# Writing out the order of the first batch's groups as a list in a fused attention and router kernel

## The chip, the cores and the metric

The kernel runs on one core of one Trainium2 chip. The metric is the device time of one execution in microseconds (us), as the median of several executions. Five engines work side by side, each through its own instructions in the order in which they were written out: TensorE (PE, matrix products and transposes, with its weight loads shown apart as PEld), VectorE (DVE), ScalarE (ACT), GpSimd (POOL) and SyncE (SP, which here only issues transfers). An engine that reaches an instruction whose inputs are not ready waits there, and everything behind it on that engine waits too.

## The reference, cut to what matters

```python
def phi(x):                       # S1, S2: 8 x 32 sketches
    a = einsum('rd,bhsd->bhsr', S1, x)
    b = einsum('rd,bhsd->bhsr', S2, x)
    return (a[..., :, None] * b[..., None, :]).reshape(..., 64)

q_p, k_p = phi(q), phi(k)         # batch 4, heads 4, sequence 1088, head size 32
kv = einsum('bhsf,bhsd->bhfd', k_p, v)
z = k_p.sum(axis=2)
attn = (q_p @ kv) / (q_p . z + 1e-6)

x = attn as 4352 rows of 128      # the heads of a token side by side
logits = normed(x) @ normed(expert_emb).T / tau       # 8 experts
e, gate = argmax and softmax's maximum of logits
out[row] = gate[row] * (relu(x[row] @ w1[e]) @ w2[e])  # w1: 128 x 1024, w2: 1024 x 128
```

Attention has no softmax: the keys and values of a head are first summed into one 64 x 32 matrix, so all keys have to be through before the first query is answered. Each row then goes through one of eight experts.

## The kernel before, in words

**Two halves.** The batch of four is taken in two halves of two (`m` = 0 and 1; the names of the steps of the first half end in 0, "ktr0"). A half has 17 tiles of 128 positions. They are taken in groups of four, called 0 to 3, and a last tile of one, called r. The changed lines are about the first half alone. What a group goes through, step by step:

- `ktr0 g`, `qtr0 g` (helper `turned`): PE transposes the group's keys or queries, four 128x128 transposes into one of two PSUM buffers of the name `ps_t`, and ACT copies the result to SBUF (kT, qT; rows of line 377).
- `kab0 g` (helper `sketch`, line 394): PE multiplies the turned keys by both sketches into the PSUM bank `ps_ab`. `kb0 g` (line 400): ACT copies the second factor out. `kp0 g` (helper `features`, line 410): DVE multiplies the two factors, 128x1024 numbers.
- `pairs g` (line 558): for the queries PE computes the two factors already repeated as the 64 products need them, into two PSUM buffers `ps_big`, of which there are exactly two. The 16 products of a group write both buffers in turn, the first buffer first. `sec g 0`, `sec g 1` (function `seconds`, line 567): ACT copies the second factors of each buffer to SBUF, 128x512 each. `prod g 0`, `prod g 1` (function `prods`, line 570): DVE multiplies the first factors, still in PSUM, by the copied second ones into `held`. The next group's `pairs` can write a buffer only when the `prod` on it is done.
- `kv0 g` (line 472): PE sums the products of keys and values in the PSUM bank `ps_acc`.
- The last tile r has short forms of these: `kab0 r`, `kb0 r`, `kp0 r` for the keys, `qab0 r`, `qb0 r`, `qp0 r` for the queries.

**Steps that belong to no group.** `constants` (DVE memsets), `sketches` (`turn_sketches`), `iotas` (POOL writes index tables, DVE converts them in eleven instructions, lines 282 to 302; they serve the router later), `norm emb` and `scale emb` (the norm of the expert embeddings: ACT squares, POOL takes the root by a power, DVE scales and lays them out, lines 318 to 334), `clear 0` and `clear 1` (POOL zeroes the two `kz` tiles, line 310), and `ktr 0`, the first turned keys of the second half.

**What sets the order.** Nothing is planned by a scheduler: within `emit` the functions are called in an order that is fixed by numbers. `put_at(tick)` returns `put(after, rank, f)`, which files the function f under the tick plus `after`, and `emit` calls all of a tick in order of rank. Group i of the first half is filed around tick i; from tick 4 on the list `ORDER` names the steps one by one, and the expert blocks follow from tick 10. The ranks of the first half's groups come out as this order before the change:

```
constants; ktr0 0; sketches; qtr0 0;
kab0 0; kb0 0; pairs 0; sec 0 0; ktr0 1; sec 0 1; kp0 0; qtr0 1; prod 0 0; prod 0 1;
kab0 1; kb0 1; pairs 1; sec 1 0; ktr0 2; sec 1 1; kp0 1; qtr0 2; prod 1 0; prod 1 1; iotas; clear 0;
kab0 2; kb0 2; pairs 2; sec 2 0; ktr0 3; sec 2 1; kv0 0; kp0 2; qtr0 3; prod 2 0; prod 2 1; kv0 1; ktr0 r; qtr0 r; norm emb; clear 1;
kab0 3; kab0 r; kb0 3; kb0 r; pairs 3; qab0 r; sec 3 0; qb0 r; sec 3 1; scale emb; ktr 0; kp0 3; kp0 r; prod 3 0; prod 3 1; qp0 r; kv0 2;
kv0 3; kv0 r;  then ORDER: tremb; total0; ktr 1; trkv0; ...
```

`tremb` turns the scaled embeddings (PE) and lays them out in `en_blk` (`place_emb`, DVE, line 344); `kve0` (line 496) is the first product that needs `en_blk`; from it come the columns of `kz` that give a query its logits (`nd 0 0` and on, line 610).

Of the kernel before, what the change touches and what calls it, by code (L numbers as in the profile page):

```python
# [27 lines left out]
NC = S // HALF  # L28
# [37 lines left out]
def kernel(  # L66
# [242 lines left out]
    def clear(m):  # L309
        nc.gpsimd.memset(kz[m], 0.0)  # L310
# [40 lines left out]
    TABLE1 = 12  # L351


    ORDER = """
tremb; total0; ktr 1; trkv0; kvT0; kab 0 ab; kb 0; trqp0r; kve0; kab 1 acc; kz0; ktr 2; nd 0 0; kb 1; ktr 3;
kp 0; nd 0 1; kab 3 ab; kb 3; x 0 0; nd 0 2; kab 2 t; x 0 1; kp 1; x 0 2; kb 2; kp 3; kv 0; nd 0 3; ktr r;
# [8 lines left out]
    steps = {}  # L365
# [19 lines left out]
    def sketch(ps, t, n):  # L385


        for h in range(H if n > 1 else 1):
            for u in range(2):
                r = slice(u * HALF, (u + 1) * HALF)  # L390
                if n == 1:
                    nc.tensor.matmul(ps[r, :H * 2 * R], t[:, r], Sblk.rearrange("p g r -> p (g r)"), start=True, stop=True)
                else:
                    nc.tensor.matmul(ps[r].rearrange("p (g h r) -> p g h r", h=H, r=2 * R)[:, :, h],  # L394
                                     t[:, h * P + u * HALF:h * P + (u + 1) * HALF], Sblk, start=True, stop=True)
        return ps[:, :n * H * 2 * R].rearrange("p (g t r) -> p g t r", t=2, r=R)
# [18 lines left out]
    def ab_bank(tick, n, u):  # L415


        if (tick, n) not in ab_ps:
            if n == 1:
                ps = ps_small()[:, :2 * n * HALF].rearrange("p (u n) -> p u n", u=2)  # L420
            else:
                ps = ps_one("ab").rearrange("p (u n) -> p u n", u=2)
            ab_ps[tick, n] = ps
        return ab_ps[tick, n][:, u, :n * HALF]

    def ab_next(kind, n, bank):

        if n == 1:
            return ab_ps[kind][:, 4 * HALF:5 * HALF]
        ab_ps[kind] = ps_small() if bank == "t" else ps_one(bank)  # L430
        return ab_ps[kind][:, :n * HALF]
# [2 lines left out]
        for bank in ("ab", "acc", "t"):  # L434
            steps[f"{name} {bank}"] = lambda bank=bank: f(bank)

    def keys(m, c0, c1, put=None):
        n = c1 - c0
        s = {}

# [1 line left out]
            s["kT"] = turned(None if n == 1 else k_sb[m][:, :, c0:c0 + 4], k_rest[m], n, "kT")  # L442

        def ab(bank=None):
            s["ab"] = sketch(ab_bank(put.tick, n, 1) if put else ab_next("k", n, bank), s["kT"], n)

        both = m == 1
        by_pool = m == 1 and c0 > 0
# [53 lines left out]
        if m == 1:  # L502
# [3 lines left out]
            if n == 1:  # L506
                steps.update({"total": total, "trkv": tr_kv, "kvT": kvT, "kve": lambda: kve(0), "kz": lambda: kve(1)})
            return
        put(-1, 50.6 if n > 1 else 55.5, tr)
        put(0, 49.8, ab)  # L510
        put(0, 49.85, b)
        put(0, 53, prod)
        first = c0 >= NC - 5
        put(*((2, 51) if c0 == 0 else (1, 47) if first else (1, 55)), kv)
        if c1 == NC:
            steps.update({"total0": total, "trkv0": tr_kv, "kvT0": kvT, "kve0": lambda: kve(0), "kz0": lambda: kve(1)})

    xg, lg, spare, turned_q = {}, {}, {}, {}

    def queries(m, c0, c1, put=None):  # L520
        n = c1 - c0
        w = n * P
        s = {}
# [9 lines left out]
            s["qT"] = turned(None if n == 1 else q_sb[m][:, :, c0:c0 + 4], q_rest[m], n, "qT")  # L533

        def ab(bank=None):
            s["ab"] = sketch(ab_bank(put.tick, n, 0) if put else ab_next("q", n, bank), s["qT"], n)

        both = m == 1

# [23 lines left out]
        def seconds(j):  # L563
            if j == 0:
                s["b"] = tile_of(n, [P, 2, w], "qpT")
                s["qpT"] = held[:, c0 // 4].rearrange("p (a n) -> p a n", a=2)
            nc.scalar.copy(s["b"][:, j], s["big"][j].rearrange("p j n -> p (j n)")[:, 2 * P:6 * P])

        def prods(j):
            nc.vector.tensor_mul(s["qpT"].rearrange("p a (j n) -> p j a n", j=4)[:, 2 * j:2 * j + 2],  # L570
                                 bview(s["big"][j], [[6 * P, 2], [P, 2], [1, P]]),
                                 s["b"][:, j].rearrange("p (j a n) -> p j a n", j=2, a=2))
# [60 lines left out]
        if n > 1:  # L633
            steps.update({f"nd {m} {step}": nd, f"x {m} {step}": x})
        if m == 0:
            put(-1, 53 if n > 1 else 55.6, tr)
            if n == 1:
                put(0, 50, ab)
                put(0, 50.5, b)
                put(0, 54, prod)  # L640
                steps.update({"trqp0r": tr_qp, "qpT0r": qpT})
            else:
                put(0, 50, pairs)
                for j in range(2):
                    put(0, 50.5 + 0.2 * j, lambda j=j: seconds(j))
                    put(0, 54, lambda j=j: prods(j))
        else:
            steps.update({f"qtr {step}": tr, f"qb {step}": b, f"qp {step}": prod,
                          f"trqp {step}": tr_qp, f"qpT {step}": qpT})
            by_bank(f"qab {step}", ab)  # L650
# [390 lines left out]
    def put_at(tick):  # L1041
        def put(after, rank, f):
            at.setdefault(tick + after, []).append((rank, len(at.get(tick + after, ())), f))
        put.tick = tick
        return put

    for i, group in enumerate(GROUPS):
        for tiles in group:
            for m in range(NM):
                keys(m, *tiles, put_at(i) if m == 0 else None)  # L1050
                queries(m, *tiles, put_at(i) if m == 0 else None)
    put_at(-1)(0, 40, more_constants)
    put_at(-1)(0, 52.9, turn_sketches)
    put_at(1)(0, 55, iotas)
    put_at(2)(0, 60, norm_emb)
    put_at(3)(0, 51, scale_emb)
    put_at(3)(0, 52, steps["ktr 0"])
    put_at(1)(0, 91, lambda: clear(0))
    put_at(2)(0, 91, lambda: clear(1))

    count, rest, others = plan_early()
    find, high, low, sums, tokens, *_ = table(0, 1, lambda: early["key"])
# [120 lines left out]
```

## Time and profile before

| what | us |
|---|---|
| median of 3 executions | 207.26 (206.97 to 208.28) |
| profiled execution, its own time | 206.99 |
| its span, first to last instruction | 205.2 |
| PE busy, share of the span | 194.0, 95% |
| ACT busy | 103.0, 50% |
| DVE busy | 87.8, 43% |
| POOL busy | 106.8, 52% |
| start of the first transposes (`ktr0 0`) | 4.34 |
| `tremb`, first step of ORDER | 24.71 |
| first gather of rows for the experts (POOL) | 50.13 |

The profile shows one execution. Each row of its timeline gives the start, the length, the engine, the line and the tiles of an instruction or of several alike, and in brackets how long its engine had sat idle before it and what ended that wait. Matrix products are pipelined, so rows of PE overlap by some tenths of a us; starts are the better guide. The chain of work that ended last is followed back from the last instruction; each piece of it is what the next one waited for. The core's granted TensorE clock has a mean of 0.998 of full speed, so a changed clock is no theme of the profile before.

The first 25 us hold the first half's groups. Loads of k, q and v fill the transfer engines from 4.5 us on (busy shares of 0.95 to 1.15 between 4.5 and 25 us), issued by SP without a wait on any computation.

### The profile page before, as it was taken

Reading aid. Unit: us, or ns where it says so; the run is one execution under the profiler, and the core shown is the slowest. Engines: PE = TensorE matmul, PEld = TensorE weight load, DVE = VectorE, ACT = ScalarE, POOL = GpSimd, SP = SyncE. Lnnn points to the kernel's source line nnn. Section 1 sums busy time; section 2 is a strip of 40 time slices with the busy share of each in tenths; the row PEclk is TensorE's granted clock in tenths of the full one; section 3 lists DMA queues with packets and bytes.
Section 4 is the critical chain, followed back from the end, with each engine's and each line's share of the span. In section 5 each row is a group of like instructions: output and inputs, shape, how many; then the busy total and the mean of one; then the engine's idle time right before and its main releaser. Section 6 shows DMA issues by size and latency. Waiting matters only on the chain.

```text
span 205.2 us, 6948 instructions
## 1 busy us (share of the span) xinstructions
PE 194.0 (95%) x2586; PEld 183.3 (89%) x2586; DVE 87.8 (43%) x378; ACT 103.0 (50%) x294; POOL 106.8 (52%) x137
## 2 busy tenths in 40 slices
PE   7989998999897999999999999999999999998991
PEld 7658788798787999999999999999999999997891
DVE  6577847788948368931221312212122122122100
ACT  2656461436373546534654555546555465776330
POOL 4010035302743567666777767677676776753033
PEclk9999999999999999999999999999999999999999
DMA  4999899568354996645465665665656794592000
GB/s 132 334 274 315 179 311 292 165 221 248 70 216 136 318 341 175 184 155 154 146 199 177 165 210 156 181 196 154 210 161 176 229 313 152 200 268 114 3 26 24
DMA packets 28162, 39.42 MB, mean 192 GB/s; under 512 B 5738, under 2 KB 21366, under 8 KB 28130
## 3 DMA queue, kind: packets, MB, share of 16 engines
q1 hardware_dynamic: 25776, 34.23, 56.7%
q0 software_dynamic: 2304, 4.74, 7.6%
q8 instruction: 22, 0.36, 0.7%
q14 instruction: 10, 0.08, 0.1%
q10 hardware_dynamic: 50, 0.01, 0.0%
HBM read 34.37 MB, written 4.73 MB: 191 GB/s over the span
## 4 chain that ended last, share of the span: by engine, by line
PE 88%; DVE 3%; ACT 2%; DMA 2%; issue 2%; POOL 0%; POOLq 0%; DVEq 0%
PE ps_big L983 27%; PE ps_acc L1019 14%; PE ps_ab L1019 14%; PE ps_acc L472 4%; PE ps_big L610 4%; PE ps_big L988 4%; PE ps_t L375 4%; DMA xs<-rows,dst_i 2%; PE ps_t L935 2%; PE ps_big L558 2%; PE ps_acc L1022 2%; PE ps_ab L1022 2%; PE ps_t L801 2%; PE ps_acc L105 1%; PE ps_ab L394 1%
## 5 line engine op out<-in xcount | busy, mean ns | idle before, releaser
L983 PE MATMUL ps_big<-xTb,wb 128*128 128x128 f32 x512 | 62.8, 276 | 0.0
L1031 POOL DMA_INDIRECT out_dram<-y,dst_i x36 | 37.5, 1043 | 44.4 <-ACT sq L996 20.1
L983 PEld LDWEIGHTS ps_big<-xTb,wb 128*128 128x128 f32 x512 | 59.7, 192 | 0.5 <-issue 0.2
L991 ACT ACTIVATE hT<-ps_big 128x1024 f32<-128x1024 f32 x36 | 36.8, 1024 | 37.2 <-PE ps_big L983 36.4
L929 POOL DMA_INDIRECT xs<-rows,dst_i x36 | 37.6, 1043 | 18.9 <-DVE dst_i L816 10.9
L937 DVE COPY xTb<-ps_t 128x128 f32<-128x128 f32 x29 | 8.4, 291 | 61.9 <-PE ps_t L935 61.9
L1019 PE MATMUL ps_acc<-w_sb,hT 128*128 x256 | 31.3, 275 | 0.1
L1019 PE MATMUL ps_ab<-w_sb,hT 128*128 x256 | 31.2, 275 | 0.0
L1019 PEld LDWEIGHTS ps_acc<-w_sb,hT 128*128 128x128 f32 x256 | 29.9, 192 | 0.1
L1019 PEld LDWEIGHTS ps_ab<-w_sb,hT 128*128 128x128 f32 x256 | 29.9, 192 | 0.0
L997 POOL TENSOR_TENSOR norm<-norm,half_c 128x1 f32<-128x1 f32 x36 | 21.3, 595 | 3.6 <-ACT sq L996 3.0
L1010 DVE TENSOR_SCALAR gate<-gate 128x1 f32<-128x1 f32 x36 | 5.5, 152 | 22.1 <-ACT probs L1007 22.0
L1028 ACT ACTIVATE y<-ps_acc,gate 128x128 f32<-128x128 f32 x18 | 6.6, 367 | 14.3 <-PE ps_acc L1019 10.9
L410 POOL TENSOR_TENSOR kp<-both 128x1024 f32<-128x1024 f32 (+1 forms) x4 | 6.5, 1619 | 11.8 <-ACT both L405 10.8
L1028 ACT ACTIVATE y<-ps_ab,gate 128x128 f32<-128x128 f32 x17 | 6.2, 367 | 10.3 <-PE ps_ab L1019 8.7
L996 ACT ACTIVATE sq<-xs 128x128 f32<-128x128 f32 x36 | 10.9, 302 | 1.0 <-DMA xs<-rows,dst_i 0.9
L1007 ACT ACTIVATE probs<-xs,norm 128x8 f32<-128x8 f32 x36 | 10.6, 295 | 1.3 <-DVE norm L1001 1.3
L935 PE MATMUL ps_t<-ident,xs 128*128 128x128 f32 x36 | 10.2, 282 | 0.9 <-DMA xs<-rows,dst_i 0.9
L472 PE MATMUL ps_acc<-v,kp 128*64 128x64 f32 x256 | 9.4, 225 | 0.7 <-issue 0.5
L472 PEld LDWEIGHTS ps_acc<-v,kp 128*64 128x64 f32 x256 | 8.3, 138 | 1.6 <-issue 1.2
L377 ACT COPY kT<-ps_t 128x512 f32<-128x512 f32 (+1 forms) x10 | 5.2, 524 | 7.6 <-PE ps_t L372 3.8
L988 PE MATMUL ps_big<-xTb,wb 128*64 128x64 f32 x128 | 7.8, 223 | 0.0
(246 smaller groups left out, 291.2 us busy)
## 6 DMA issues: line engine op xcount, KB each, us to landing
wb<-in_moe_w_dram SPq DMA_DIRECT2D x36, 512.0 KB, 4.8
w_sb<-in_moe_w_dram SPq DMA_DIRECT2D x16, 256.0 KB, 4.8
rows<-xg SPq DMA_DIRECT2D x4, 544.0 KB
v<-in_v_dram SPq DMA_DIRECT2D x4, 512.0 KB
v<-in_moe_w_dram SPq DMA_DIRECT2D x4, 512.0 KB
k<-in_k_dram SPq DMA_DIRECT2D x3, 512.0 KB
q<-in_q_dram SPq DMA_DIRECT2D x3, 512.0 KB
xs<-rows,dst_i POOLq DMA_INDIRECT x36, 3.5
```

Source lines behind the costliest of these rows:

```text
L472: nc.tensor.matmul(acc[m][u * HALF:(u + 1) * HALF, i, p], s["kp"][:, c - c0, h], bass.AP(tensor=vo.tensor, offset=vo.offset, ap=[list(vo.a ...
L929: nc.gpsimd.indirect_dma_start(out=xs[i][:], out_offset=None, in_=rows[:2 * S if t == 0 else N + 1], in_offset=bass.IndirectOffsetOnAxis(a ...
L935: nc.tensor.transpose(ps[:, :P], xs[i][:, :DM], ident)
L983: nc.tensor.matmul(ps[:, u, j * P:(j + 1) * P], w[:, f * P:(f + 1) * P], x, start=True, stop=True)
L988: nc.tensor.matmul(ps[r, u, j * P + b * HALF:j * P + (b + 1) * HALF], wh[:, f * P + c * HALF:f * P + (c + 1) * HALF], x[:, b * HALF:(b + 1 ...
L991: nc.scalar.activation(hT[i], ps, ACT.Relu)
L996: nc.scalar.activation(sq, xs[i][:, :DM], ACT.Square, accum_out=norms[i])
L997: nc.gpsimd.tensor_tensor(out=norms[i], in0=norms[i], in1=half_c, op=ALU.pow)
L1007: nc.scalar.activation(p, xs[i][:, DM:], ACT.Exp, scale=norms.pop(i)[:, 0:1], accum_out=gate[i])
L1019: nc.tensor.matmul(ps, h[:, f * P:(f + 1) * P], ws[0][:, f], start=f == 0, stop=f == NF - 1)
L1028: nc.scalar.activation(y, ps, ACT.Copy, scale=gate.pop(i)[:, 0:1])
L1031: d = nc.gpsimd.indirect_dma_start(out=out[:, :], out_offset=bass.IndirectOffsetOnAxis(ap=dst_i[t][:, j:j + 1], axis=0), in_=y[:], in_offs ...
```

## The change

The ranks of the first half's steps are gone. Each step now has a name, a new list `HEAD` gives their order, and one loop files them all under tick 0. `ORDER` and everything behind it are as they were. Read engine by engine, the new list differs from the old order thus:

- ACT: in each round `sec g 1` stands directly behind `sec g 0`, ahead of the copies of the next turned keys and queries; before, the copy of the turned keys stood between them. In the last round both stand ahead of the short copies of tile r.
- DVE: the eleven conversions of `iotas` stand behind all of the first half's products and behind `scale emb`, ahead of `place_emb`; before, they stood between rounds 1 and 2. `scale emb` stands behind `qp0 r`; before, it stood ahead of `kp0 3`.
- PE: `kv0 0` stands behind `qtr0 3`, `kv0 1` behind `pairs 3` and the transposes of tile r, and the short products of tile r follow it; before, `kv0 0` and `kv0 1` stood around `qtr0 3`, and tile r's products around `pairs 3`.
- POOL: `clear 0` comes first, then the power of `norm emb`, then all the index tables, then `clear 1`; before, two of the tables, then the others and `clear 0`, then the power and `clear 1`.

No instruction is added or taken out, and no transfer is touched.

```diff
@@ ahead of ORDER
+    HEAD = """
+constants; ktr0 0; sketches; qtr0 0; kab0 0; kb0 0; pairs 0; kp0 0; sec 0 0; sec 0 1; ktr0 1; qtr0 1; prod 0 0;
+prod 0 1; kab0 1; kb0 1; pairs 1; kp0 1; sec 1 0; sec 1 1; ktr0 2; qtr0 2; prod 1 0; prod 1 1; kab0 2; kb0 2; pairs 2;
+kp0 2; sec 2 0; sec 2 1; ktr0 3; qtr0 3; prod 2 0; prod 2 1; clear 0; kv0 0; kab0 3; kb0 3; pairs 3; kp0 3; sec 3 0;
+sec 3 1; ktr0 r; qtr0 r; prod 3 0; prod 3 1; kv0 1; norm emb; kab0 r; kb0 r; qab0 r; qb0 r; kp0 r; qp0 r; scale emb;
+iotas; clear 1; ktr 0; kv0 2; kv0 3; kv0 r
+"""
@@ keys (queries likewise)
-    def keys(m, c0, c1, put=None):
+    def keys(m, c0, c1, tick=None):
...
-            s["ab"] = sketch(ab_bank(put.tick, n, 1) if put else ab_next("k", n, bank), s["kT"], n)
+            s["ab"] = sketch(ab_bank(tick, n, 1) if m == 0 else ab_next("k", n, bank), s["kT"], n)
...
-        put(-1, 50.6 if n > 1 else 55.5, tr)
-        put(0, 49.8, ab)
-        put(0, 49.85, b)
-        put(0, 53, prod)
-        first = c0 >= NC - 5
-        put(*((2, 51) if c0 == 0 else (1, 47) if first else (1, 55)), kv)
+        g = name_of(c0)
+        steps.update({f"ktr0 {g}": tr, f"kab0 {g}": ab, f"kb0 {g}": b, f"kp0 {g}": prod, f"kv0 {g}": kv})
@@ queries
-            put(-1, 53 if n > 1 else 55.6, tr)
+            steps[f"qtr0 {step}"] = tr
             if n == 1:
-                put(0, 50, ab)
-                put(0, 50.5, b)
-                put(0, 54, prod)
+                steps.update({"qab0 r": ab, "qb0 r": b, "qp0 r": prod})
...
-                put(0, 50, pairs)
+                steps[f"pairs {step}"] = pairs
                 for j in range(2):
-                    put(0, 50.5 + 0.2 * j, lambda j=j: seconds(j))
-                    put(0, 54, lambda j=j: prods(j))
+                    steps[f"sec {step} {j}"] = lambda j=j: seconds(j)
+                    steps[f"prod {step} {j}"] = lambda j=j: prods(j)
@@ where the steps are filed
-                keys(m, *tiles, put_at(i) if m == 0 else None)
-                queries(m, *tiles, put_at(i) if m == 0 else None)
-    put_at(-1)(0, 40, more_constants)
-    put_at(-1)(0, 52.9, turn_sketches)
-    put_at(1)(0, 55, iotas)
-    put_at(2)(0, 60, norm_emb)
-    put_at(3)(0, 51, scale_emb)
-    put_at(3)(0, 52, steps["ktr 0"])
-    put_at(1)(0, 91, lambda: clear(0))
-    put_at(2)(0, 91, lambda: clear(1))
+                keys(m, *tiles, i)
+                queries(m, *tiles, i)
+    steps.update({"constants": more_constants, "sketches": turn_sketches, "iotas": iotas, "norm emb": norm_emb,
+                  "scale emb": scale_emb, "clear 0": lambda: clear(0), "clear 1": lambda: clear(1)})
+    for i, name in enumerate(x.strip() for x in HEAD.split(";")):
+        put_at(0)(0, i, steps[name])
```

## The prediction

> **What bounds the kernel now.** I read the busy shares first: PE is busy for 194.0 of 205.2 us, so a change counts only where it moves PE. Then the chain that ended last, in order of time, for the first 25 us, the only part that the change touches. It runs through PE, save in rounds 1 and 2, where it changes between PE and ACT (start, length, what):
>
> ```profile
> 10.62 1.37 PE ps_big L558 x27
> 11.99 0.02 issue
> 12.01 0.60 ACT qpT L567
> 12.61 0.04 issue
> 12.65 0.40 ACT kT L377
> 13.05 0.08 issue
> 13.13 0.59 ACT qpT L567
> 13.72 0.50 ACT qT L377
> 14.22 0.04 issue
> 14.26 1.35 PE ps_big L558 x27
> ```
>
> The reader sees one whole round: `pairs 1`, then four copies in a row on ACT (`sec 1 0`, kT, `sec 1 1`, qT), then `pairs 2`. PE has no other work meanwhile than four key transposes, four query transposes and `kab`. From 14.26 on PE is without a wait until `tremb` at 24.71.
>
> Second, the timeline of PE, rows of line 558, one for each round:
>
> ```profile
> 7.25 1.12 PE L558 MATMUL ps_big<-qT,S_pairs 32*64 32x256 f32 x32
> 10.62 1.34 PE L558 MATMUL ps_big<-qT,S_pairs 32*64 32x256 f32 x32 [0.29 <-ACT qT L377]
> 14.26 1.35 PE L558 MATMUL ps_big<-qT,S_pairs 32*64 32x256 f32 x32 [0.29 <-ACT qT L377]
> 19.98 1.12 PE L558 MATMUL ps_big<-qT,S_pairs 32*64 32x256 f32 x32
> ```
>
> The same 32 instructions last 1.12 us in rounds 0 and 3 and 1.35 in 1 and 2. The timeline of DVE and the busy time of line 558 in short stretches (stretch, length, then PE's and PEld's busy time with instructions) say why:
>
> ```profile
> 10.11 0.69 DVE L570 TENSOR_TENSOR held<-ps_big,qpT 128x512 f32<-128x512 f32 x1 [0.35 <-ACT qpT L567]
> 13.75 0.69 DVE L570 TENSOR_TENSOR held<-ps_big,qpT 128x512 f32<-128x512 f32 x1 [0.43 <-ACT qpT L567]
> 10.70:10.85 0.15, 0.15 (x2) 0.11 (x4) 1.00 1.04 335
> 10.85:11.00 0.15, 0.15 (x10) 0.15 (x14) 1.00 1.11 355
> ```
>
> `prod 0 1` ends at 10.80 and `prod 1 1` at 14.44. `pairs` starts at 10.62, but until about 10.8 only two instructions run; then ten. The first products go to the first `ps_big`, the next to the second, which `prod n 1` still reads. So `pairs` stalls in its middle, without a row that says so, because `sec n 1`, and `prod n 1` behind it, came one ACT slot late.
>
> **The main part, rounds 0 to 2.** Let T be the start of `sec n 0`: 8.45, 12.01, 15.66 now, so rounds of 3.56 and 3.65. T of round 0 stays, since nothing ahead of it changes order on PE, ACT or DVE. The new round, step by step:
>
> - ACT starts copies of this size 0.48 apart when nothing is awaited (9.00, 9.48, 9.96): `sec n 1` at T+0.48, kT at T+0.96, qT at T+1.44. Now kT stands at T+0.55 to 0.64 and qT at T+1.51 to 1.59.
> - From kT's start to `kab` it is 0.64 (9.00 to 9.64, 12.65 to 13.28): `kab` at T+1.60. Now it is at T+1.2: this is the price of the move, 0.4 us, paid in PE's gap ahead of `kab`, which grows from 0.30 to about 0.65.
> - `kab` needs 0.46 to 0.51 before the next product can follow (31.13 to 31.59, 19.25 to 19.76), so T+2.10. qT is ready 0.66 after its start (9.96 to 10.62), T+2.10 too. The gap of 0.29 that stands ahead of `pairs` now is gone: `pairs` at T+2.10 instead of T+2.17 (round 0) and T+2.25 (round 1).
> - `prod n 0` starts 0.62 after T, `prod n 1` 0.60 behind it (two of them took 1.28 at 17.97) and ends at T+1.91, ahead of `pairs`. No stall: from `pairs` to the next T it is 1.20 (7.25 to 8.45) instead of 1.39 and 1.40.
>
> The new round is 2.10 + 1.20 = 3.30. Two rounds: (3.56 - 3.30) + (3.65 - 3.30) = **0.61 us gained**, 0.39 from the stall and 0.22 from the gaps. Next late is DVE: `kb` moves behind `kab` to T+2.31, `kp` to T+2.64 and its end to T+3.87, where the next `prod` wants DVE at T+3.92. It fits by 0.05; were it late, `prod n 1` would still be done 0.19 ahead of `pairs`.
>
> Both ends: if `pairs` keeps its 1.40 for a reason I don't see, the round is 3.50 and the gain 0.21. If ACT's copies come 0.60 apart (8.45 to 9.00 and 12.01 to 12.65 are 0.55 and 0.64), kT is at T+1.20 and the round 3.54, a gain of 0.13; with both, 3.74, a loss of 0.27. I take 0.48, because three copies in a row show it and the wide ones waited for transposes that ended beside them (8.97, 12.55).
>
> **Round 3 and the sums on PE.** With T now 15.05 for round 2, PE's next work has no gap, from the starts of before: `ktr0 3` 0.59, `qtr0 3` 0.58, `kv0 0` 1.08 (covers the copies: kT done at T+1.56, `kab0 3` starts at T+2.13), `kab0 3` 0.51, `pairs 3` 1.05, transposes of r 0.37, `kv0 1` 1.09, `kab0 r` and `qab0 r` 0.48 (the copies of r end at T+5.2, this starts at T+5.15), `ktr 0` 0.59, `kv0 2` and `3` 2.27, `kv0 r` 0.56: `tremb` at T+9.05 = 24.10 against 24.71. Moved sums cost nothing as long as loads are there: everything here that a load feeds starts within 0.7 us of its start before, and `kv0 0`, the tile r and `kv0 1` start no more than 0.1 earlier or even later.
>
> **The conversions on DVE.** They took from 14.36 to 16.84, 2.48 us. Taken from between rounds 1 and 2 they gain nothing: `kp0 2` was late behind them, but PE ran the sums meanwhile without a gap. At their new place they stand ahead of `place_emb`:
>
> ```profile
> 25.04 0.29 DVE L344 TENSOR_TENSOR en_blk<-ps_big,mask 128x32 f32<-128x32 f32 x2
> 26.59 0.33 PE L496 MATMUL ps_t<-en_blk,kvT 128*128 128x64 f32 x2
> ```
>
> `en_blk` was there 1.26 us before its use. New: `qp0 r` ends at T+6.5, the scaling takes 1.3 (20.66 to 21.98), the conversions 2.5, `place_emb` 0.3: T+10.6. `kve0` stands at T+9.05+1.88 = T+10.93. It fits by 0.3. Ends: with the eleven lengths added up without overlap (3.15 us) `en_blk` is at T+11.3 and PE waits 0.35; below, nothing is gained. I take no cost, as they ran overlapped before. On POOL the tables now queue behind the power of `norm emb`, and `clear 1` behind the tables, which wait for DVE; POOL's next work behind it starts only at 29.16, four us later. SP's queue has nothing moved.
>
> A lock could spoil this. POOL's tables and zeroing ran beside these same conversions at 14.65 to 15.30, in 0.25, 0.18 and 0.38 us, against 0.25 and 0.36 for a table at 2.86 and `clear 1` at 20.59: at most 0.02 longer. The Trainium skill, "SBUF — State Buffer", section "Who interferes with whom", speaks against the move: a conversion in DVE's two-port mode and a GpSimd instruction exclude one another for a whole instruction. By that rule some 0.8 us of POOL's work would be added to DVE's, `kve0` would wait 0.5 and only 0.1 of the gain would be left; by the rows it is nothing.
>
> **The sum.** Profiled execution 206.99 - 0.61 = 206.4. Its own time lies 0.27 below the median 207.26. The list behind `kv0 r` is the same and PE is its chain up to the first gather at 50.13, so the shift should travel. For a median I say **206.6**, between 206.4 and 207.26 - 0.61 = 206.65.
>
> **The rivals.**
>
> *The stall stays, or the copies are slower* (15 in 100). For it: no row names the wait inside `pairs`. Against: both resumptions lie within 0.05 us of a `prod`'s end. Gain 0.1 to 0.2, time 207.0.
>
> *The gain is swallowed behind* (17 in 100). The twelve loads of w2 issue from 24.00 to 35.28 whatever the computation does, and the first gather took 4.92 us against a median of 3.5. For it: transfers were 0.92 busy from 30 to 40 us. Against: the chain has the gather released by `dst_i` on DVE, and from 40 to 50 us transfers were at 0.73. Time 207.2.
>
> *Slower: `en_blk` becomes the last to come* (14 in 100). The chain is `emb_sq` on ACT, now behind six copies of round 3, the power on POOL (0.58), the scaling, the conversions, `place_emb`. It costs PE what it is late beyond T+10.93, and decides when it is over 0.94 late, more than slack and gain together, that is if `emb_sq` starts after T+6.4 or the conversions wait for POOL's tables. A late `en_blk` also delays `nd 0 0` and everything that needs a logit. Priced with POOL's own 0.8 and the 0.65 of unoverlapped lengths: 0.8 + 0.65 - 0.94 = 0.5 slower, 207.8.
>
> *As forecast*: 54 in 100, 206.3 to 206.9. The range takes in the rivals and half a us of scatter at the lower end (three executions lay 206.97 to 208.28): 205.9 to 207.9. A difference of under 1%, 2.07 us, is about what a measurement of this kernel can't tell from no change. No case here reaches it: 3 in 100 for faster, where a shifted gather meets fewer transfers, 4 for slower, 93 within.
>
> **What the profile will show.** If right: `pairs 1` and `pairs 2` in 1.12 us, starting near 10.55 and 13.85; one gap of 0.65 ahead of each `kab` and none ahead of `pairs`; `sec 2 0` near 15.05; `tremb` near 24.1; `en_blk` ending near 25.7, before `kve0` at 26.0; the gather near 49.5. If wrong: `pairs` still 1.35, a wait of PE for `en_blk`, or a gather that starts earlier and lands no earlier. The time is wrong if the shift at `tremb` doesn't reach the last store.

## The result and the profile after

The changed kernel took 208.15 us in the median of 22 runs (206.82 to 212.54), the kernel before 207.4 on the same chip (22 runs, 206.72 to 210.79): a ratio of 1.0017, with an interval of 0.9992 to 1.0041. Ratios, here and below, leave out executions in a slower state of the chip (here 212.54 on one side and 210.79 on the other), so they aren't the quotients of the medians. No difference can be told. The profiled execution of the changed kernel took 208.19 us (span 206.4), 1.20 more than the one of before (206.99), and the mean granted clock of its TensorE was 0.990 instead of 0.998.

The first 25 us look much as forecast. The chain that ended last, in order of time (start, length, what), for round 1 and the beginning of round 2:

```profile
9.53 0.69 PE ps_ab L401 x16
10.22 1.05 PE ps_big L561 x32
11.27 1.04 PE ps_t L382 x8
12.30 0.61 ACT kT L384
12.91 0.04 issue
12.96 0.69 PE ps_ab L401 x16
```

Of ACT's four copies in the round only kT is left in the chain; before, all four stood in it. Line 401 is now the line of `kab` and 561 that of `pairs`. The timeline of PE (in brackets the idle time before a row and what ended it):

```profile
6.72 1.12 PE L561 MATMUL ps_big<-qT,S_pairs 32*64 32x256 f32 x32
9.53 0.69 PE L401 MATMUL ps_ab<-Sblk,kT 128*64 128x64 f32 x16 [0.66 <-ACT kT L384]
10.15 1.12 PE L561 MATMUL ps_big<-qT,S_pairs 32*64 32x256 f32 x32
12.96 0.69 PE L401 MATMUL ps_ab<-Sblk,kT 128*64 128x64 f32 x16 [0.67 <-ACT kT L384]
13.57 1.12 PE L561 MATMUL ps_big<-qT,S_pairs 32*64 32x256 f32 x32
17.19 1.12 PE L561 MATMUL ps_big<-qT,S_pairs 32*64 32x256 f32 x32
20.30 0.34 PE L399 MATMUL ps_t<-Sblk,qT 128*64 128x64 f32 x4 [0.28 <-ACT kb L407]
23.64 0.28 PE L340 MATMUL ps_big<-ident,emb 8*128 8x8 f32 x2
25.24 0.44 PE L591 MATMUL ps_t<-ident,qp 128*128 128x128 f32 x2
25.64 0.41 PE L503 MATMUL ps_t<-en_blk,kvT 128*128 128x64 f32 x2
25.98 0.69 PE L401 MATMUL ps_acc<-Sblk,kT 128*64 128x64 f32 x16
32.32 1.10 PE L479 MATMUL ps_acc<-v,kp 128*64 128x64 f32 x32
34.40 0.46 PE L613 MATMUL ps_big<-kz,qpT 128*64 128x82 f32 x8
...
55.70 3.56 PE L984 MATMUL ps_big<-xTb,wb 128*128 128x128 f32 x16 [1.21 <-ACT xTb L938]
```

`pairs` takes 1.12 us in every round and nothing is waited for ahead of it; there is one gap of 0.66 ahead of `kab`. The row of 20.30, with a wait of 0.28 for `kb0 r`, had no counterpart before and none in the forecast. `tremb` (line 340) is at 23.64, 1.07 earlier than before. The rows from 25.24 on belong to what is told below; the row of 55.70 is the first product of the first expert block.

The timeline of DVE and ACT shows `place_emb` behind the moved conversions (22.75 to 25.22, 2.47 us, 2.48 before), and two rows of a later stage:

```profile
25.22 0.28 DVE L344 TENSOR_TENSOR en_blk<-ps_big,mask 128x32 f32<-128x32 f32 x2
...
55.35 0.17 DVE L626 TENSOR_SCALAR rc<-ps_big 128x16 f32<-128x16 f32 x1 [2.53 <-PE ps_ab L591]
55.38 0.27 ACT L938 COPY xTb<-ps_t 128x128 f32<-128x128 f32 x1 [3.46 <-PE ps_ab L591]
```

`en_blk` ends at 25.50 and its first user, `kve0` (line 503), starts at 25.64. No row of the timeline names a wait there, but the starts show one. The same rows before, with the later ones that the two profiles are compared by below:

```profile
26.32 0.44 PE L588 MATMUL ps_t<-ident,qp 128*128 128x128 f32 x2
26.86 0.69 PE L394 MATMUL ps_acc<-Sblk,kT 128*64 128x64 f32 x16
33.20 0.46 PE L472 MATMUL ps_acc<-v,kp 128*64 128x64 f32 x9
36.01 0.51 PE L610 MATMUL ps_big<-kz,qpT 128*64 128x82 f32 x8
```

Before, with `en_blk` there for long, `kve0` (26.59) started 0.27 us behind the two transposes ahead of it, and the next row 0.27 behind `kve0`. Now it is 0.40 and 0.34: PE goes on 0.20 us later. As rows of PE overlap, a wait of this size leaves no gap between them. That it is `en_blk` that is waited for, a kernel below shows by name.

Where the 1.20 us of the two profiled executions come from is read by counting each stage from the one before. T is the start of `sec 0 0`; "placement" is the first sum of the second half's placement (line 702, now 703), "block 30" and "block 35" the transposes of these expert blocks. All in us:

| stage | before | after | difference |
|---|---|---|---|
| start to T | 8.45 | 7.92 | -0.53 |
| T to `tremb` | 16.27 | 15.72 | -0.55 |
| `tremb` to the first gather | 25.42 | 24.83 | -0.59 |
| first gather to placement | 14.60 | 17.44 | +2.84 |
| placement to block 30 | 106.62 | 106.58 | -0.04 |
| block 30 to block 35 | 21.88 | 21.94 | +0.06 |
| block 35 to the end | 11.98 | 11.99 | +0.01 |
| outside the span | 1.79 | 1.79 | 0 |

Up to `tremb` the front is 0.55 shorter, and the stages ahead of T and from `tremb` to the first gather are 1.1 shorter together, for reasons told below; then 2.84 is lost at one place. The busy time in stretches of 1 us (stretch, length, PE, PEld, DVE, ACT and POOL with instructions, granted clock, transfers' share, GB/s) shows it:

```profile
54.00:55.00 1.00, 0.49 (x5) 0.26 (x3) 0.00 (x0) 0.00 (x0) 0.49 (x1) 1.00 1.05 159
55.00:56.00 1.00, 0.30 (x1) 0.30 (x2) 0.58 (x3) 0.61 (x2) 0.00 (x0) 0.74 0.71 287
56.00:57.00 1.00, 1.00 (x6) 1.00 (x6) 0.96 (x3) 0.93 (x4) 0.00 (x0) 0.50 0.90 295
59.00:60.00 1.00, 1.00 (x23) 0.83 (x23) 0.00 (x0) 0.70 (x1) 0.00 (x0) 1.00 0.28 70
```

From 55.48 to 58.89, that is for 3.41 us, TensorE had half its clock. (In seven of the 13 profiles the last 0.4 to 2.2 us are at half clock as well, behind PE's last products; alone, that makes a mean of 0.994 to 0.999.) The row of 55.70 took 3.56 us in it; the same 16 products took 1.79 in the chain of a later execution of the same kernel. Ahead of it PE stood still for 1.21 us, waiting for the copy of 55.38 on ACT, which started 3.46 us after ACT's work before it; DVE's row of 55.35 started as late, after 2.53 us. The question for the experiments was therefore double: is the gain of the front real, and is the loss behind it the change's doing?

### The profile page after: what moved, and what is told of

It is laid out like the page before. It is cut to its first block, busy times and chain, and to the rows that moved or that the text cites. A ratio compares the mean times of both kernels' runs of the same rounds, so it can differ in the third digit from the quotient of the medians.

```text
span 206.4 us, 6948 instructions
## 1 busy us (share of the span) xinstructions
PE 194.8 (94%) x2586; PEld 183.9 (89%) x2586; DVE 88.0 (43%) x378; ACT 102.9 (50%) x294; POOL 107.0 (52%) x137
## 4 chain that ended last, share of the span: by engine, by line
PE 88%; DMA 3%; DVE 3%; ACT 2%; issue 1%; POOL 0%; POOLq 0%; DVEq 0%
PE ps_big L984 28%; PE ps_acc L1020 14%; PE ps_ab L1020 14%; PE ps_big L989 4%; PE ps_acc L479 4%; PE ps_big L613 4%; PE ps_t L382 4%; DMA xs<-rows,dst_i 2%; PE ps_t L936 2%; PE ps_ab L401 2%; PE ps_big L561 2%; PE ps_acc L1023 2%; PE ps_ab L1023 2%; PE ps_t L802 1%; ACT qpT L570 1%
## 5 line engine op out<-in xcount | busy, mean ns | idle before, releaser
L984 PE MATMUL ps_big<-xTb,wb 128*128 128x128 f32 x512 | 64.4, 280 | 1.2 <-ACT xTb L938 1.2
L984 PEld LDWEIGHTS ps_big<-xTb,wb 128*128 128x128 f32 x512 | 61.2, 196 | 1.9 <-ACT xTb L938 1.4
L1008 ACT ACTIVATE probs<-xs,norm 128x8 f32<-128x8 f32 x36 | 10.6, 295 | 1.2 <-DVE norm L1001 1.2
L319 POOL TENSOR_TENSOR emb_ss<-emb_ss,half_c 8x1 f32<-8x1 f32 x1 | 0.6, 577 | 17.0 <-ACT emb_sq L318 17.0
L479 PE MATMUL ps_acc<-v,kp 128*64 128x64 f32 x256 | 8.9, 224 | 0.0
L989 PE MATMUL ps_big<-xTb,wb 128*64 128x64 f32 x128 | 8.3, 224 | 0.3 <-issue 0.2
```

Of the source, the lines that this page charges most:

```text
L479: nc.tensor.matmul(acc[m][u * HALF:(u + 1) * HALF, i, p], s["kp"][:, c - c0, h], bass.AP(tensor=vo.tensor, offset=vo.offset, ap=[list(vo.a ...
L984: nc.tensor.matmul(ps[:, u, j * P:(j + 1) * P], w[:, f * P:(f + 1) * P], x, start=True, stop=True)
L989: nc.tensor.matmul(ps[r, u, j * P + b * HALF:j * P + (b + 1) * HALF], wh[:, f * P + c * HALF:f * P + (c + 1) * HALF], x[:, b * HALF:(b + 1 ...
L1008: nc.scalar.activation(p, xs[i][:, DM:], ACT.Exp, scale=norms.pop(i)[:, 0:1], accum_out=gate[i])
```

## The experiments

**The theory**: the new order shortens the front by what its two parts bring (second factors ahead, and the rest of the list), and this reaches the end; what hides it differs from one execution to the next and has nothing to do with the order. **The rivals**: the gain is swallowed between `tremb` and the end; the new order itself brings TensorE to half its clock by a longer idle time ahead of the first expert block; or the list, apart from its order, costs something.

In the edits below, marked lines are those of `HEAD`, cut to what differs. Four kernels ran on one chip, four on a second, three on a third, each beside the kernel before; the chip of the result above is a fourth.

### The old order as a list

```diff
-constants; ktr0 0; sketches; qtr0 0; kab0 0; kb0 0; pairs 0; kp0 0; sec 0 0; sec 0 1; ktr0 1; qtr0 1; prod 0 0;
...
+constants; ktr0 0; sketches; qtr0 0;
+kab0 0; kb0 0; pairs 0; sec 0 0; ktr0 1; sec 0 1; kp0 0; qtr0 1; prod 0 0; prod 0 1;
+kab0 1; kb0 1; pairs 1; sec 1 0; ktr0 2; sec 1 1; kp0 1; qtr0 2; prod 1 0; prod 1 1; iotas; clear 0;
...
```

> The kernel before, its order written as a list: the instructions of each engine are those of the kernel before, so this is a second and independent look at it, and the scale for the others. All theories: ratio 1.000, with rounds at 3.56 and 3.65 us and pairs 1 and pairs 2 at 1.35 us each. Theory A (a lower granted clock near the first gather is a matter of the new order): no stretch at half clock between 50 and 62 us, gather's rows used at about 55 us. Theory B (it is an accident that either order meets in some executions): such a stretch may show here as well, and single executions scatter by 1 to 2 us with it.

Measured: 205.0 us against 204.64, ratio 1.0015 (0.9991 to 1.004). T to `tremb` is 16.27, as before. Its instructions are those of the kernel before, so its ratio also shows what a comparison of like with like gives: 0.15% off.

### The change once more, on the same chip

The kernel is the changed one, without an edit.

> The changed kernel once more. Both theories: the front as in its first profile, rounds of 3.42, tremb 0.5 to 1.0 us earlier than in the kernel before of the same chip, the gather 0.5 to 1.6 us earlier. Theory A (the gain is lost again each time, since PE falls to half clock near the first gather): a stretch of 3.4 us at clock 0.5 between 52 and 60 us again, time 0 to 0.4% above the kernel before. Theory B (accident): no such stretch in this profile or one in either kernel, and a span 0.4 to 0.8 us under that of the kernel before.

Measured: 204.75 us against 204.64, ratio 1.0008 (0.9977 to 1.0039); its profiled execution took 204.17. T to `tremb` 15.72 again, the first gather 40.61 and placement 55.18 from T, and no half clock between 50 and 62 us: what cost the first profile 2.84 us isn't there. So the order alone doesn't bring it.

The two profiles side by side also show where T comes from. The timeline of PE of the old order as a list, and of the changed kernel:

```profile
5.48 1.00 PE L383 MATMUL ps_t<-ident,q 128*128 128x128 f32 x4
```

```profile
5.55 0.66 PE L382 MATMUL ps_t<-ident,q 128*128 128x128 f32 x4
```

The same four transposes, ahead of anything that the change moves, take 1.00 us in the one and 0.66 in the other, and T is 8.35 and 8.07. Over all 13 profiles T follows the moment of the trace's first entry on TensorE's clock, whatever the kernel: first entry at 4.28 us, T 7.92; 5.28, 7.94; 5.59, 8.07; 6.23, 8.35; 6.72, 8.45; 7.05, 8.55; 7.35, 8.69. That spread of 0.78 us is more than the whole forecast gain.

### Each part alone

Second factors ahead, everything else in the old order:

```diff
-kab0 1; kb0 1; pairs 1; sec 1 0; ktr0 2; sec 1 1; kp0 1; qtr0 2; ...
+kab0 1; kb0 1; pairs 1; sec 1 0; sec 1 1; ktr0 2; kp0 1; qtr0 2; ...
```

> One part alone: in the old order only the second copy of second factors is moved directly behind the first, in all four rounds; tables and sums stay. If the stall inside pairs is cured by this part alone: pairs 1 and pairs 2 in 1.12 us, rounds of 3.42, tremb 0.36 us earlier than in the kernel before. If the conversions between rounds 1 and 2 matter for PE after all, less. Whole time: Theory A 0 to 0.3% slower than or equal to the kernel before, theory B 0.2% faster.

The new list, with the second factors put back between the turned tiles:

```diff
-kab0 1; kb0 1; pairs 1; kp0 1; sec 1 0; sec 1 1; ktr0 2; qtr0 2; ...
+kab0 1; kb0 1; pairs 1; kp0 1; sec 1 0; ktr0 2; sec 1 1; qtr0 2; ...
```

> The new list with the one part undone: the next turned keys are copied between the two second factors again, in all four rounds; tables' conversions behind the loop and the new places of the sums stay. Stall theory: pairs 1 and 2 at 1.35 us again, rounds of 3.6, tremb within 0.2 us of the kernel before. If the new places gained by themselves: tremb 0.2 to 0.6 us earlier in spite of the stall. Whole time within 0.2% of the kernel before.

Measured: 204.71 (ratio 0.9997, 0.9972 to 1.0023) and 205.1 (1.0024, 0.9997 to 1.0052) against 204.64. The times say nothing, the fronts do. The timeline of PE with the second factors ahead:

```profile
10.89 1.12 PE L562 MATMUL ps_big<-qT,S_pairs 32*64 32x256 f32 x32
14.32 1.12 PE L562 MATMUL ps_big<-qT,S_pairs 32*64 32x256 f32 x32
```

and with all the rest of the change but that:

```profile
14.33 1.35 PE L562 MATMUL ps_big<-qT,S_pairs 32*64 32x256 f32 x32 [0.29 <-ACT qT L385]
```

The stall inside `pairs` goes and comes with the place of `sec n 1` and with nothing else. With the second factors alone the three starts of T are 8.66, 12.09 and 15.51: rounds of 3.43 and 3.42 instead of 3.56 and 3.65, 0.36 gained, and T to `tremb` is 15.88. With the rest alone the rounds stay at 3.57 and 3.64, but from round 2's T to `tremb` it is 8.77 instead of 9.05, and T to `tremb` 15.98: 0.29 gained where the forecast had nothing. Together they bring 0.55, not quite the sum of 0.39 and 0.29.

But `tremb` is not the end of what the change moves. Behind it, with the rest of the change alone, the timeline of PE and that of DVE:

```profile
26.09 0.44 PE L592 MATMUL ps_t<-ident,qp 128*128 128x128 f32 x2
26.82 0.41 PE L504 MATMUL ps_t<-en_blk,kvT 128*128 128x64 f32 x2 [0.29 <-DVE en_blk L344]
26.39 0.28 DVE L344 TENSOR_TENSOR en_blk<-ps_big,mask 128x32 f32<-128x32 f32 x2
```

Here the wait for `en_blk` is named. `kve0` starts 0.73 behind the two transposes, and 0.15 behind the end of `en_blk`; in the changed kernel that is 0.14. The step behind it starts at 27.16, so PE goes on 0.53 us later than it would (0.73 + 0.34 against 0.27 + 0.27). With the second factors alone, the conversions at their old place, it is 0.28 and 0.26 as before. So the moved conversions do cost, and the fixed point has to lie behind them. Counted to the sums near 33 us (line 472 before: 33.20, 24.75 from T), the second factors alone gain 0.39 (24.36), the rest alone loses 0.24 (24.99), and both together gain 0.34 or 0.35 (24.40 to 24.42). The second factors alone are better there than the whole change.

### Two more profiles of the change

The changed kernel, without an edit, one execution each.

> The changed kernel, a further profile. Measured from the first second-factor copy, both profiles so far have the first gather at 40.6 us (the old order 41.4 and 41.7). Theory C (the front's gain is real, and waits in the last blocks that differ from one execution to the next hide it): gather again at 40.6, the first placement sum of the second half at 55.2 when no half clock falls in, and a wait of PE of 0.2 to 1.5 us near 188 us. Theory D (the new order loses its gain in some executions between tremb and the first expert block): a gather or a placement sum later than 41.2 and 55.8 in one of the two looks, with a wait or a half clock that shows it.

> The same kernel again. Theory C and theory D as for the first look; two looks tell how often.

Measured: 204.36 and 205.29 us; the kernel before took 204.57 there (23 runs). T to `tremb` 15.72 in both, no half clock between 50 and 62 us. The second was 0.34 later at placement: its PE waited 0.5 us near 33 us for nothing that the profile names ("issue"). The first had such a wait later, in its chain:

```profile
187.29 0.28 issue
187.57 1.22 PE ps_acc L1023 x17
```

The profile before has the same wait at the same work, 1.50 us long (the chain, line 1022 then), and one of 0.52 at 33.65:

```profile
33.65 0.52 issue
...
188.82 1.50 issue
190.32 1.09 PE ps_acc L1022 x16
```

Counted along PE's own stream of records (weight loads, products and PE's other instructions), these waits stand at records 705, 1217, 5057 and 5313, or one or two further, in all profiles that have them: each is 193 more than a multiple of 256. Most such places show no wait. Two rows of "issue" stand elsewhere, 0.17 and 0.18 us long, both in the first profile of the changed kernel. The queue that brings instructions to the engines (queue, kind, packets, MB, share) says what comes in such steps; the line is the same in every profile:

```profile
q8 instruction: 22, 0.36, 0.7%
```

22 packets of 16 KB, and PE's stream has 5,579 records: some 256 to a packet. In the profile before, one packet was under way from 31.35 to 32.57 and PE went on at 34.17; another from 187.90 to 188.92, and PE went on at 190.32. In all 18 waits at these records, over the 13 profiles, PE restarts 1.2 to 1.6 us after a packet's end, so the wait is long or short by how late that packet was fetched. Why it is fetched late in one execution and early in another stays open.

### The queries' short product ahead of `kb0 r`

```diff
-kab0 r; kb0 r; qab0 r; qb0 r;
+kab0 r; qab0 r; kb0 r; qb0 r;
```

> The new list with one pair swapped: tile r's query products stand directly behind its key products, ahead of the copy kb0 r. In the new list they stand behind that copy, and both products share one PSUM tile, so PE sits idle for 0.28 us (qab0 r behind kb0 r). If that wait is on the path: no such wait, tremb 0.3 us earlier counted from the first second-factor copy (15.4 instead of 15.7), and the whole time 0.15% under the changed kernel's 1.0008 if the scatter of the rest lets it be seen. If something else is late there: tremb unchanged.

Measured: 204.65 against 204.57, ratio 1.0011 (0.9984 to 1.0038). The wait of 0.28 is gone, as the timeline of PE shows, and another one has come:

```profile
20.32 0.34 PE L399 MATMUL ps_t<-Sblk,kT 128*64 128x64 f32 x4
20.49 0.34 PE L399 MATMUL ps_t<-Sblk,qT 128*64 128x64 f32 x4
20.76 0.66 PE L382 MATMUL ps_t<-ident,k 128*128 128x128 f32 x4
...
22.36 1.67 PE L479 MATMUL ps_acc<-v,kp 128*64 128x64 f32 x50 [0.34 <-issue]
```

From `kab0 r` to `ktr 0` it is 0.44 instead of 0.89 (19.68 to 20.57 in the profile after). So the two short products are kept apart because `kb0 r` on ACT stood between them, over the tile that they share. But at record 705 PE waited 0.34 for an instruction packet in this execution, and `tremb` came 15.88 after T instead of the 15.4 that was expected. A wait of this kind is no part of the order: the last kernel below has it at the same row.

### TensorE kept busy ahead of the first expert block

Four products of zeros, 128 by 128, are added ahead of the first gathered tile's transpose; nobody reads their result.

```diff
+    def stay_warm(n):
+        ps = ps_one("acc")
+        for _ in range(n):
+            nc.tensor.matmul(ps[:, :P], zeros[:, :P], zeros[:, :P], start=True, stop=True)
...
-"turn 0": lambda: turn(0)
+"turn 0": lambda: (stay_warm(4), turn(0))
```

> The new order with four more 128x128 products of zeros on PE just ahead of the first block's transpose, whose results nobody reads: they fill some 0.9 us in which PE waits for the first gather. Theory A (idle PE near the gather brings the half clock and costs the gain): no stretch at half clock between 50 and 62 us and 0.2 to 0.4% faster than the kernel before. Theory C: time as that of the changed kernel, 0.999 to 1.001.

Measured: 205.55 against 204.57, ratio 1.0024 (1.0001 to 1.0046): above what either theory expected, and no gain. Since the changed kernel showed no half clock near 55 us on these chips without the zeros either, this doesn't tell whether they would keep it away on the chip of the result. The profiled execution (207.43) has none near 55 us, but one at 189. The busy time in stretches (as above):

```profile
187.00:188.70 1.70, 0.00 (x0) 0.00 (x0) 0.32 (x2) 0.50 (x3) 0.00 (x0) 1.00 0.01 1
188.70:189.00 0.30, 0.29 (x6) 0.29 (x8) 0.00 (x0) 0.00 (x0) 0.00 (x0) 1.00 0.00 0
189.00:190.00 1.00, 1.00 (x16) 1.00 (x14) 0.00 (x0) 0.00 (x0) 0.00 (x0) 0.52 0.00 0
```

PE stood 1.70 us for an instruction packet, and 0.3 us after it had gone on, with work for many us behind it, its clock was halved for 3.41 us. Block 30 to block 35 took 23.71 us here, 20.2 to 21.9 elsewhere.

### The third chip: old order, new order, and a shifted stream

The old order as a list and the changed kernel again, both without a further edit; and the changed kernel with 24 products of zeros, 16 by 16, ahead of the first gathered tile (nobody reads them), so that everything behind stands 96 records later in PE's stream.

```diff
+    def small_ones(n):
+        ps = ps_one("acc")
+        for _ in range(n):
+            nc.tensor.matmul(ps[:2 * R, :2 * R], zeros[:, :2 * R], zeros[:, :2 * R], start=True, stop=True)
...
-"turn 0": lambda: turn(0)
+"turn 0": lambda: (small_ones(24), turn(0))
```

> The old order as a list once more, on one chip with the changed kernel. Theory C (the front's gain is real; PE's waits for its own instructions and the moment at which the clock is released scatter by more than it): counted from the first second-factor copy, tremb at 16.27 as in the two profiles before; the first copy itself anywhere between 7.9 and 8.7 us, by when the clock was released; a PE wait for nothing that the profile shows at 33.5 us or near 188 us, of 0 to 1.9 us. Ratio 1.000 within its interval.

> The changed kernel on the same chip. Theory C: tremb at 15.72 counted from the first second-factor copy, 0.55 under the old order; the medians of the two within 0.3% of each other, with the best execution of the new order 0.1 to 0.6 us under the best of the old one. Theory D (the new order brings losses of its own): the new order's best execution is no better than the old one's, or a wait shows that no profile of the old order has.

> The new order with 24 products of 16x16 zeros on PE ahead of the first block's transpose, while PE waits for the first gather: 96 more records on PE from there on, results unread. If the late wait of PE belongs to a place in its stream of instructions (record 5313 in the profiles so far, 705 and 1217 earlier, 512 or a multiple of it apart), it stays at record 5313 and so comes 96 records earlier in the work, in the first layer of a block instead of its second (about 3 us earlier than 187.5). If it belongs to the operation or to a transfer, it stays in the second layer, at record 5409.

Measured: the old order 205.51 against 205.26, ratio 1.0001 (0.9973 to 1.0028); the new order 204.81, ratio 0.9971 (0.9946 to 0.9995); the shifted one 205.51 in its one execution. The fastest executions were 204.36 (the list), 204.05 (the kernel before) and 204.06 (the new order), so the lead of the best one that was expected shows against the list alone. T to `tremb` is 16.27 in the old order, 15.72 in the new one. In the shifted one it is 16.14; PE's wait at record 705, the one that the kernel with `qab0 r` ahead showed, stands in that stretch (22.52). It shows as 0.15 of idle time, but `tremb` is 0.42 later than without it: rows of PE overlap, so a wait costs some 0.2 us more than the idle time that it shows as, and a short one shows none. The chain of the shifted one:

```profile
185.27 1.04 PE ps_big L989 x34
186.31 0.38 issue
186.69 1.09 PE ps_big L989 x29
```

The wait is at record 5313 still, but it fell in the second layer's products (line 1023) in the profiles above and falls in the first layer's here. In this execution it thus belongs to a place in the stream, not to an operation or to what is loaded for it.

### What the profiles say together

The wait near 33 us falls between two rows that both timelines above show: the first of the sums (`ps_acc<-v,kp`) and the first product with `kz,qpT`. From start to start it is 2.08 us where PE doesn't wait; what is above is the wait's whole price.

| kernel | T to `tremb` | T to the sums | sums to `kz,qpT` | T to the first gather | the same without the wait | T to placement | profiled time |
|---|---|---|---|---|---|---|---|
| before | 16.27 | 24.75 | 2.81 | 41.68 | 40.95 | 56.29 | 206.99 |
| old order as a list | 16.27 | 24.75 | 2.53 | 41.39 | 40.94 | 55.78 | 205.02 |
| the same, third chip | 16.27 | 24.75 | 2.42 | 41.29 | 40.95 | 55.89 | 206.29 |
| second factors alone | 15.88 | 24.36 | 2.97 | 41.44 | 40.55 | 56.41 | 205.71 |
| the rest alone | 15.98 | 24.99 | 2.08 | 41.12 | 41.12 | 55.61 | 206.12 |
| changed, the result's profile | 15.72 | 24.40 | 2.08 | 40.55 | 40.55 | 57.99 | 208.19 |
| changed, same chip as the list | 15.72 | 24.40 | 2.10 | 40.61 | 40.59 | 55.18 | 204.17 |
| changed, second chip | 15.72 | 24.41 | 2.27 | 40.79 | 40.60 | 55.31 | 204.36 |
| changed, second chip again | 15.72 | 24.42 | 2.74 | 41.27 | 40.61 | 55.66 | 205.29 |
| changed, third chip | 15.72 | 24.42 | 3.33 | 41.87 | 40.62 | 56.23 | 206.24 |

Without the wait the first gather comes 40.94 to 40.95 after T in the old order and 40.55 to 40.62 in the new one: 0.35 earlier. Of the 0.55 at `tremb` 0.20 is lost again at `kve0`, and 0.35 is what the change brings. The second factors alone bring 0.40, and the rest alone loses 0.17. Of the other three kernels with the new order, the one with `qab0 r` ahead has 40.58 by this count, the one with four products of zeros 40.59, and the shifted one, with its wait at record 705, 40.82.

Behind the gather nothing more depends on the order, as far as the profiles show. The gathered rows take 4.72 to 5.33 us until their first transpose, in no relation to the order; from there to placement it is 9.64 to 9.66 us, save in the result's profile (12.62) and in the kernel with four products of zeros (9.76); from placement to block 30 it is 106.57 to 106.65 us in all 13. So the first rival is right in part: 0.20 of the gain is swallowed, right behind `tremb`, by the change's own move of the conversions. The third falls, with ratios of 1.0015 and 1.0001 for the list that holds the old order.

The three measurements of the changed kernel, 1.0017, 1.0008 and 0.9971, weighted by their intervals, give 0.9997 with about 0.0015 to either side. The forecast gain, 0.61 us of 206, would be 0.9970, and lies outside; 0.35 us would be 0.9983, just inside, and so is no gain at all. The times thus don't show the gain, the profiles do. The first and the third interval hardly meet, so one interval isn't the whole spread from chip to chip.

The second rival, half clock, is settled in part. On the chip of the result 10 of the 22 executions of the changed kernel had a mean clock of at most 0.992, which is what one stretch of 3.41 us at half clock gives (1 - 3.41 x 0.5 / 206); their median was 208.38 us, that of the other 12 was 207.89. On the other chips none of the 24 executions of the changed kernel that were timed had it, and none of 105 of the old order. The clocks of the old kernel's executions on the chip of the result, except the profiled one, weren't recorded, so whether the new order falls into it more often there stays open. Without those ten the median is still not below 207.4.

## Why the prediction was right, and where its steps were off

That no difference could be told was the likeliest case by far, and it came; it would have come with no gain at all as well, so it says little for the steps. The 206.6 was not reached: at 1.0017 of 207.26 the time is 207.6, inside the range and 1.0 above the forecast. The gain that the profiles show is 0.35 us where 0.61 was forecast. Step by step:

- **The stall inside `pairs`**: right, in its cause and its size. `pairs` takes 1.12 us in each round, and only the place of `sec n 1` decides it.
- **The round of 3.30**: mis-sized, it is 3.42 and 3.43. The term is `kab` to `pairs`, "0.46 to 0.51 before the next product can follow", taken as 0.50. It measured 0.62 and 0.61 (9.53 to 10.15, 12.96 to 13.57). The rows that gave 0.46 to 0.51 stood behind other work of PE without a gap; this `kab` stands behind a wait, and so did those of the kernel with the second factors alone (10.28 to 10.89). `kab0 3`, without a gap ahead, took 0.57 in the same profile. Two rounds gained 0.14 and 0.22, 0.36 instead of 0.61.
- **Round 3 and the sums, "T+9.05"**: 8.87 (14.77 to 23.64). Two terms were off, and both are waits. `kv0 2` and `kv0 3` took 1.91, not 2.27: the 2.27 held a wait that no row of the timeline named, but that the chain of the profile before did, in lines that the forecast didn't read:

```profile
21.63 0.35 DVE emb L334 x2
21.98 1.14 DVE kp L410
23.12 0.04 issue
23.16 1.62 PE ps_acc L472 x48
```

`kv0 3` waited for `kp0 3`, which stood behind the scaling on DVE. With the rest of the list alone the two sums took 1.91 as well (22.01 to 23.92), with the second factors alone 2.28 (21.70 to 23.98): the move of `scale emb` brings 0.36 that the forecast hadn't seen. Against it stands **a new wait**: `kab0 r` and `qab0 r` took 0.89, not 0.48, because `qab0 r` now comes right behind `kb0 r` and waits 0.28 for it. The rest, some 0.2, is in shorter steps of `ktr0 3`, `qtr0 3` and `kv0 0`. "From 14.26 on PE is without a wait" and a chain that "runs through PE, save in rounds 1 and 2" were thus wrong.
- **The front's sum**: 0.55 against 0.61 at `tremb`. Two errors of opposite sign nearly cancel: 0.25 less from the rounds, 0.18 more from round 3.
- **The conversions at no cost**: wrong, and it costs nearly as much as the mis-sized rounds. The conversions took 2.47 us, as forecast, but the slack of 0.3 wasn't there, and PE lost 0.20 at `kve0`. `qp0 r` ended at T+6.88 (21.65), not T+6.5, as DVE waited 0.61 us for ACT's short copies, `qb0 r` the last of them, which stands behind the new wait, so `en_blk` ended at T+10.73 instead of T+10.6. PE was ready for it at T+10.74 (25.51, 0.27 behind the transposes of 25.24) instead of T+10.93, as `tremb` came earlier than forecast. And the forecast set the end of `en_blk` against the start of `kve0`, where 0.14 us lie between the two in the profiles that wait. The rival "`en_blk` becomes the last to come" was thus true in part, at 0.20 instead of the 0.5 at which it was priced.
- **The shared port**: POOL's tables and zeroing lay beside the conversions again (23.03 to 23.68) and took 0.25, 0.18 and 0.38 us, the lengths of before. That doesn't speak against the rule that the Trainium skill gives under "SBUF — State Buffer", "Who interferes with whom", since DVE can be the one that is held up. DVE's row of line 285 took 0.49 us in either order and ended 0.07 behind POOL's zeroing (15.37 and 15.30 before, 23.75 and 23.68 after), while the cast of line 282, with as many columns, took 0.22. A lock would thus be in the 2.48 us of before already. No run has these conversions without POOL beside them, so it stays open.
- **"T of round 0 stays"**: true of the order, not of the executions. T is 7.91 to 8.69 by the moment of TensorE's first clock entry. This is the step that made 206.6 more exact than it could be.
- **"The shift should travel"**: 0.35 of the 0.55 does, past the first gather; the rest ends at `kve0`. **"A changed clock is no theme of the profile before"** was true of that profile and was carried over to the next, which has 3.41 us at half clock.
- **The scatter**: half a us was allowed, from three executions. Waits for instruction packets alone show as 0 to 1.1 us of idle time near 33 us and 0 to 1.7 us between 183 and 192, over the 13 profiles.

## What to carry to other kernels

A row that is longer than its like can be a wait without a name, which the chain may show where the timeline doesn't, so both are to be read before a busy engine is called gapless; and a step that starts behind a wait is to be sized from rows that also start behind one. When an instruction is moved away from between two others, look at who shares a tile with its new neighbours. For a gain of a quarter of a percent the times decide nothing, but a stage counted from a fixed point to a fixed point shows it in one profile each, if no scattering wait lies between (here T to the sums, 24.75 in all three profiles of the old order and 24.40 to 24.42 in all five of the new one). The second point has to lie behind everything that the change can delay: at `tremb` the change seemed to bring 0.55, behind `kve0` it brings 0.35. And a change of several parts is to be measured part by part, behind the same point: here one part alone brings more than the whole.

## What the runs showed of the hardware

- PE waits for its own instructions: at places that lie a multiple of 256 records apart, up to 1.7 us long, shown as "issue" in the middle of a run of products, with the restart 1.2 to 1.6 us after the end of a 16 KB packet on the instruction queue. Shifting the stream by 96 records left the wait at its record and gave it to other work.
- A wait of PE can leave no gap between its rows: `kve0` came 0.13 us late behind `en_blk` in the profile after, and the wait near 33 us cost the old order 0.34 us on the third chip, without idle time in either place; in the profile before, 0.52 us of idle time shows where 0.73 was lost.
- In the middle of two profiles TensorE's clock is halved, for 3.41 us each time. It came after about 1.80 us of idle time of PE in the 3.41 us ahead (the profile after, at 55.48) and after 1.72 (the kernel with four products of zeros, at 189.03); 1.50 of idle time at 188.82 in the profile before brought none.
- The Trainium skill, "TensorE: Matmul & The Clock Gate", "Part 1: The HAM clock gate (the "warmup" mystery)", gives a free-running window of 3413 ns and half clock after at least one idle window. The length agrees; "idle" doesn't have to mean that PE does nothing in it, as PE was at work for about half of either window here.
- In the profile after, and in no other, DVE and ACT started two reads after 2.53 and 3.46 us of idle time, just ahead of the half clock, though the rows of PE that they read from end at 52.48 and 53.62. That profile also holds 2,676 records of semaphores, the others about 3,800; the cause stays open.
